# Windowed attention and gated MLP on one core: 24 small dummy products for two wide ones, and packs 2 and 3 regrouped on TensorE

## The chip, the cores and the metric

The kernel runs on one core of a Trainium2 chip, in one launch. The metric is the time of the core on the device in microseconds (us); lower is better. Engines: PE (TensorE, matrix products; PEld is its loading of weights), DVE (VectorE), ACT (ScalarE), POOL (GpSimd), SP (SyncE, which issues most DMAs).

## What is computed

Eight heads of attention over 576 positions for each of 8 batches, each query seeing a window of at most 32 keys (heads 0 to 3: the last 32 positions, heads 4 to 7: every fourth of the last 128), and a gated MLP on the result:

```python
scores = scale * np.matmul(q, k.transpose(0, 1, 3, 2))
scores = np.where(masks[None, :, :, :], scores, -1000000000.0)
scores = scores - np.max(scores, axis=-1, keepdims=True)
attn = np.exp(scores)
attn = attn / (np.sum(attn, axis=-1, keepdims=True) + 1e-09)
x = np.matmul(attn, v).transpose(0, 2, 1, 3).reshape(B * S, H * D)
g = x @ w_gate
out = (g * (1 / (1 + np.exp(-g))) * (x @ w_val)) @ w_out
```

## The kernel before

Attention is cut into packs (PACKS; 4 heads, two times 4 blocks of 32 queries with 64 keys each), numbered m from 0. A pack goes through `scores` (two mask products in bf16, then 32 fp32 products of a 64x32 corner of PE, which the profile shows as 64 records), `shift` (DVE: maximum and subtraction), `exps` (ACT), `turn_e` (four 128x128 transposes on PE into one PSUM bank), `keys` (that bank copied to SBUF, by DVE for the packs in KEYS, else by ACT), `results` (32 fp32 products with v, 64 records), `norm` and `turn_y` (DVE), and `x_copies`, which split the result into two float32r parts (upper by ACT, lower by POOL or DVE) as input x of the MLP.

The MLP goes by items: 256 or 512 tokens by 128 of the 1536 inner columns. An item has 12 gate products (`gv_mm(it, 0)`, bank bg), 12 value products (`gv_mm(it, 1)`, bank bv) and 12 output products (`out_mm`, banks bo0 to bo3); its activation runs on ACT, DVE and POOL. The weights come as 64-bit numbers; each half of an f is loaded by SP, taken apart on ACT and DVE and split into an upper part (ACT cast) and a lower part (POOL, or DVE for the units in W_LOW), unit by unit, while PE works. The first three chunks of 512 tokens are done this way (the first, up to f = 2, as two halves of 256); the rest by a scheme with fewer products, which the change doesn't touch.

The order of the work has two parts. START (line 68) is a hand-written string for the first 16 us: Q are scores, S shift, X exps, T transposes, K keys, A results, N norm, U turn_y, H and L the copies of x, w the loads of weights, W a step of them; I and J are dummy products on a tile of ones, whose output nobody reads (`idle`, lines 812 to 820). After it a recording layer (class Desk, lines 164 to 322) takes down what the loop over the items calls and issues it: PE keeps the order of the calls, the other engines' instructions are ordered by a model of costs and due times, so a change on PE reorders them too. Where in the loop a pack's steps are called stands in EARLY and LATER: three slots for A (results of the pack before, scores of this one), B (transposes and keys) and C (`x_copies`); an item t has slots 3t, 3t + 1 and 3t + 2. Packs 2, 3 and 4 have the rows of EARLY (line 65). All instructions of START show as line L234, those of the recorded part as L250.

```python
EARLY = (-1, 1, None), (2, 4, 3), (5, 8, 6)
```

PE takes its instructions in this order and waits at each for its operands. `two` is the pair of PSUM banks for scores and results: scores at the end of each bank, results at its beginning.

Of the kernel before, what the change touches and what calls it, by code (L numbers as in the profile page):

```python
# [34 lines left out]
BQ = 32  # L35
# [26 lines left out]
WARM = 9  # L62
TURNED = 20
FREE = 16000, 19500, 17500, 18000, 6000
EARLY = (-1, 1, None), (2, 4, 3), (5, 8, 6)
MASKED = 6
X_LOW, W_LOW, H_LOW, KEYS = (3, 7), (1, 5), (5,), (2,)
ON_ACT = (2, 3, 4, 5, 6, 9, 11, 12, 15, 17, 19, 21, 23)
START = ("q0 q1 w v0 v1 w Q0 Q1 S0 X0 T0 W0 I3 I2 S1 K0 X1 W1 A0 W2 T1 J2 K1 W3 J2 N0 W0 w U0 q2 v2 A1 q3 w w r W4 H0 "
         "L0 N1 U1 H1 L1 W1 v3 W2 W3 W4")  # L70
LATER = (14, 3, 2), (23, 3, 4), (29, 7, 4), (39, 3, 2)
T0 = NPLAIN * CH
# [65 lines left out]
NPK = len(PACKS)  # L138
# [15 lines left out]
class Desk:  # L154
# [8 lines left out]
    LANDING, RATE, AHEAD = 2000, 373, 2000  # L163
    EARLY = 6000

# [86 lines left out]
    def issue(self):  # L252
# [7 lines left out]
        for k in range(n - 1, -1, -1):  # L260
            e, _, _, cost, later, _, _ = kept[k]
            way[k] = cost + later + (self.EARLY if later and e == 'scalar' else 0) + max((way[m] for m in after[k]), default=0)
            if e == "tensor":
# [63 lines left out]
def attention_moe(ctx, tc, qkb, vb, w, const, out):  # L327
    nc = Desk(tc.nc)
# [59 lines left out]
    ones = at(M_X0, D)  # L388
# [15 lines left out]
    STAGES = "ETBHL"  # L404
# [6 lines left out]
    def w_load(parts=2):  # L411
        nonlocal loaded
        u = loaded
        n = u % 5 if u < NU - NLAST else (u - NU + NLAST) % NRAW
        if u >= NU or raw_of.get(n, -1) >= done["B" if u < NU - 1 else "L"]:
            return False
        raw_of[n] = u
        loaded += 1
        t = at(raw_at[n], 2 * WU, I32)
        n = 2 * WU // parts  # L420
        for k in range(parts):
            nc.sync.dma_start(out=t[:, n * k:n * k + n], in_=w[u // 2, u % 2].bitcast(I32)[:, n * k:n * k + n])
        t = t.rearrange("p (n t) -> p n t", t=2)
        wst[u] = {"lo": t[:, :, 0], "hi": t[:, :, 1]}
        return True
# [4 lines left out]
    def w_exp(u):  # L430
        y = wst[u]["hi"].bitcast(F32)
        nc.scalar.activation(out=y, in_=y, func=AF.Prelu, scale=2.0 ** -112, alpha=2.0 ** 32)
# [40 lines left out]
    def w_split_hi(u):  # L473
        nc.scalar.copy(out=w_place(u)[0], in_=wst[u].bitcast(F32))
# [5 lines left out]
    ready = {"w": False}  # L480
# [10 lines left out]
    def w_one(c):  # L491
        u = done[c]
        done[c] += 1
        if c == "E":
            w_exp(u)
        elif c == "T":
            w_shift(u)
        elif c == "B":
            w_bits(u)
        elif c == "H":  # L500
            w_split_hi(u)
        else:
            w_split_lo(u)
        if c in "BL":
            while ready["w"] and w_load():
                pass
# [18 lines left out]
    def pool_of(m):  # L525
        return early if m < 2 * NSTART else later
# [24 lines left out]
    def scores(m, two, masked):  # L551

        t = st[m]["qk"]
        if masked:
            for i in range(2):
                nc.tensor.matmul(out=two[:, i, SA:].rearrange("q (g k) -> q g k", g=NG), lhsT=ident16,
                                 rhs=masks_of(m, i), start=True, stop=False, skip_group_check=True)
        for g in range(NG):
            for j in range(NH):
                for i in range(2):  # L560
                    r, q, k = slice(D * i, D * i + D), pk(m).q_at(g, j), pk(m).k_at(i, g, j)
                    nc.tensor.matmul(out=two[BQ * j:BQ * j + BQ, i, SA + BU * g:SA + BU * g + BU],
                                     lhsT=t[r, q:q + BQ], rhs=t[r, k + 1:k + BK], start=not masked,
                                     stop=not masked or g == NG - 1, skip_group_check=True)
# [27 lines left out]
    def turn_e(m, bank):  # L592
        for g in range(NG):
            nc.tensor.transpose(out=bank[:, P * g:P * g + P], in_=st[m]["e"][:, P * g:P * g + P], identity=eye)

    def keys(m, bank, pool):
        t = pool["pt"]()
        if m in KEYS:
            nc.vector.tensor_copy(out=t, in_=bank)
        else:  # L600
            nc.scalar.copy(out=t, in_=bank)
        st[m]["pt"] = t
# [126 lines left out]
    def gv_mm(it, which):  # L729

        text = "Phxw Shxw" if it.w < CH else "phxw shxw"
        if it is not items[0]:
            gv_some(it, which, gv_ops(text), True, True)
        elif which:
            gv_some(it, which, gv_ops("Shwx Phwx"), True, True)
        else:
            gv_some(it, which, gv_ops("Phwx"), True, False)
            attend(-1)
            gv_some(it, which, gv_ops("Shwx"), False, True)
# [30 lines left out]
    def out_mm(it, late=True):  # L770
        f, (_, hh, hl) = it.f, it.h
        ops = [(j, low, x) for j in range(4) for low, x in ((0, hh), (0, hl), (1, hh))]
        if not late:
            ops.sort(key=lambda o: o[2] is hl)
        for n, (j, low, x) in enumerate(ops):
            nc.tensor.matmul(out=bank_o[j][:, it.cols], lhsT=wcol(f, 2 * DM + P * j, low), rhs=x,
                             start=f == it.cols.start == low == 0 and x is hh,
                             stop=f == NF - 1 and j not in [o[0] for o in ops[n + 1:]], skip_group_check=True)
# [19 lines left out]
    two = bank_r = bank(ctx, "two", 2)  # L798
    k_bank = [bank(of_turns, x, 1, "right") for x in ("fk", "fx")] * 2
# [14 lines left out]
    def idle(n, bank=k_bank[1]):  # L814

        while n > 0:
            k = min(n, 4)
            nc.tensor.matmul(out=bank[:D, :P * k].rearrange("p (a b) -> p a b", b=D), lhsT=ones,
                             rhs=ones.unsqueeze(1).broadcast_to([P, 2 * k, D]), start=True, stop=True)
            n -= k  # L820

    idle(WARM)

    items = [Item(0, f, a, a + CH // 2) for a in (0, CH // 2) for f in range(HALVED)]
# [6 lines left out]
        "U": turn_y, "H": lambda m: x_copy(m, "hi"), "L": lambda m: x_copy(m, "lo"),  # L831
        "q": lambda m: load_qk(m, fa, nc.sync, 2),
        "v": lambda m: load_v(m, fa, nc.sync, 2),
        "w": lambda m: w_load(3), "r": lambda m: ready.update(w=True), "I": lambda n: idle(n), "J": lambda n: idle(n, k_bank[0]), "W": lambda n: w_one(STAGES[n]),
    }

    et = mybir.EngineType
# [1 line left out]
    by_hand.__enter__()  # L839
    for what in START.split():  # L840
        first[what[0]](int(what[1:] or 0))
# [14 lines left out]

    for m, x in enumerate(EARLY):
        visits(2 + m, *x)
# [18 lines left out]
    def attend(now):  # L877
        for what, m in visit.get(now, ()):
            r = ended(m)
            if what == "A":  # L880
                if r is not None:
                    results(r, two)
                if m < NPK:
                    scores(m, two, m < MASKED)
                if r is not None:
                    norm(r, two, pool_of(r))
                if m < NPK:
                    shift(m, two, pool_of(m), m < MASKED)
                if r is not None:
                    turn_y(r)  # L890
                if m < NPK:
                    exps(m)
                if 2 * NSTART <= m < TURNED:
                    load_v(m, later, nc.sync)
                elif TURNED <= m - 1 < NPK:
                    load_far(m - 1, later)
                    load_v(m - 1, later, nc.sync)
                if 2 * NSTART <= m + 1 < NPK:
                    load_qk(m + 1, later, nc.sync)
            elif what == "B":  # L900
                if TURNED <= m < NPK:
                    turn_far(m, later)
                elif m < NPK:
                    turn_e(m, two[:, 1])
                    keys(m, two[:, 1], pool_of(m))
            elif r is not None:
                x_copies(r)

# [226 lines left out]
    for t, it in enumerate(items):  # L1135
        before = items[t - 1] if t else None
        late = t >= HALVED
        if it.ci == 0:
            units(it.f)
        gv_mm(it, 0)  # L1140
        act_tanh(it)
        dve_u(it)
        attend(3 * t)
        mixing(t, 0)
        if not late and t:
            out_mm(before, False)
        gv_mm(it, 1)
        dve_h(it)
        h_hi(it)
        if not late:  # L1150
            h_lo(it)
        attend(3 * t + 1)
        if late:
            out_mm(before)
            h_lo(it)
        if t and before.f == NF - 1:
            out_store(before.ci)
        attend(3 * t + 2)
        mixing(t, 1)
        if it.ci == NPLAIN - 1:  # L1160
            if it.f >= 9:
                ask([3, 5, NAT - 1][it.f - 9])
            for n in {6: (0,), 7: (1,), 9: (2, 3), 10: (4, 5), 11: (6, 7)}.get(it.f, ()):
                x_step(n)

    for ci in range(NC):
# [20 lines left out]
        for t in range(NT):  # L1187
            for i in range(NP):
                n = n_out(ci, t, i)
# [59 lines left out]
```

## Time and profile before

| | us |
|---|---|
| median of 3 runs | 911.16 (909.72 to 911.43) |
| the profiled execution, own time | 914.47 |
| its span, first to last instruction | 912.7 |
| PE busy in the span | 897.8 (98%) |
| DVE, ACT, POOL busy | 646.0, 382.5, 257.8 |
| mean granted clock of PE | 0.996 of 2.4 GHz |

The profile is of one execution. Its page gives busy times, the DMA queues and the costliest groups of instructions; the trace behind it answers questions by stretch, engine and time. A row of a timeline merges instructions that follow each other and are alike; an fp32 product is two records, a float32r or bf16 product and a transpose one, and each record has a load of weights (PEld). "[1.89 <-issue]" behind a row is how long the engine was idle before it and what released it.

### The profile page before, as it was taken

Reading aid. Unit: us, or ns where it says so; the run is one execution under the profiler, and the core shown is the slowest. Engines: PE = TensorE matmul, PEld = TensorE weight load, DVE = VectorE, ACT = ScalarE, POOL = GpSimd, SP = SyncE. Lnnn points to the kernel's source line nnn. Section 1 sums busy time; section 2 is a strip of 40 time slices with the busy share of each in tenths; the row PEclk is TensorE's granted clock in tenths of the full one; section 3 lists DMA queues with packets and bytes.
Section 4 is the critical chain, followed back from the end, with each engine's and each line's share of the span. In section 5 each row is a group of like instructions: output and inputs, shape, how many; then the busy total and the mean of one; then the engine's idle time right before and its main releaser. Section 6 shows DMA issues by size and latency. Waiting matters only on the chain.

```text
span 912.7 us, 20897 instructions
## 1 busy us (share of the span) xinstructions
PE 897.8 (98%) x8642; PEld 737.0 (81%) x8642; DVE 646.0 (71%) x993; ACT 382.5 (42%) x593; POOL 257.8 (28%) x177
## 2 busy tenths in 40 slices
PE   6899999999999999999999999999999999999998
PEld 4798888888888888888888888888878888888886
DVE  5687779888795473777789766878787746555752
ACT  4788433333243242333336544333345533334452
POOL 2468712221311112012032630111146501213451
PEclk9899999999999999999999999999999999999999
DMA  9899986453464640887888678989866675565562
GB/s 338 326 337 368 373 287 224 153 184 122 164 239 146 211 162 13 265 288 263 291 272 282 233 247 279 306 279 296 273 211 222 212 240 198 188 199 189 193 223 92
DMA packets 90382, 214.24 MB, mean 235 GB/s; under 512 B 9264, under 2 KB 32432, under 8 KB 90288
## 3 DMA queue, kind: packets, MB, share of 16 engines
q1 hardware_dynamic: 79776, 208.09, 66.2%
q10 hardware_dynamic: 10512, 4.82, 2.0%
q8 instruction: 68, 1.11, 0.5%
q14 instruction: 26, 0.21, 0.1%
HBM read 165.69 MB, written 47.19 MB: 233 GB/s over the span
## 4 chain that ended last, share of the span: by engine, by line
PE 96%; DMA 2%; issue 1%; SPq 0%; ACT 0%; DVE 0%; POOL 0%; ACTq 0%
PE bo L250 43%; PE bg L250 23%; PE bv L250 23%; PE two L250 7%; DMA at_int<-w 1%; DMA at_float<-turned 1%; SPq L234 0%; DVE at_float L250 0%; POOL at_float32r L234 0%; ACT at_float32r L250 0%; ACT at_float32r L234 0%; ACT at_float L250 0%; ACT at_int L234 0%; ACTq L234 0%
## 5 line engine op out<-in xcount | busy, mean ns | idle before, releaser
L250 PE MATMUL bo<-at_float32r 128*128 128x512 f32 x1296 | 305.7, 390 | 0.0
L250 PEld LDWEIGHTS bo<-at_float32r 128*128 128x128 f32 x1296 | 242.6, 188 | 51.0
L250 POOL TENSOR_TENSOR at_float32r<-at_float,at_float32r 128x512 fp32r<-128x512 f32 (+1 forms) x109 | 161.0, 1480 | 388.7 <-ACT at_float32r L250 210.4
L250 ACT CAST at_float32r<-at_float 128x512 fp32r<-128x512 f32 (+2 forms) x214 | 147.9, 705 | 146.6 <-DVE at_float L250 69.9
L250 DVE TENSOR_TENSOR at_float<-bo,at_float 128x512 f32<-128x512 f32 x168 | 114.1, 683 | 99.7 <-ACT at_float L250 63.7
L250 DVE TENSOR_TENSOR at_float32r<-at_float,at_float32r 128x512 fp32r<-128x512 f32 (+1 forms) x105 | 108.9, 1051 | 48.2 <-ACT at_float32r L250 38.1
L250 PE MATMUL bv<-at_float32r 128*128 128x512 f32 x486 | 128.6, 391 | 0.0
L250 PE MATMUL bg<-at_float32r 128*128 128x512 f32 x486 | 128.3, 390 | 0.0
L250 ACT ACTIVATE at_float<-at_float 128x512 f32<-128x512 f32 (+1 forms) x108 | 67.9, 630 | 134.7 <-DVE at_float L250 121.4
L250 PE MATMUL bg<-at_float32r,at_float32r 128*128 128x512 f32 (+1 forms) x468 | 108.8, 382 | 1.8 <-ACT at_float32r L234 1.2
L250 POOL TENSOR_TENSOR at_float<-at_float,at_float 128x512 f32<-128x512 f32 x36 | 51.3, 1424 | 209.8 <-DVE at_float L250 190.8
L250 PE MATMUL bv<-at_float32r,at_float32r 128*128 128x512 f32 (+1 forms) x468 | 107.2, 379 | 0.0
L250 DVE SCALAR_TENSOR_TENSOR at_float<-at_float,at_float 128x512 f32<-128x512 f32 x144 | 106.1, 743 | 1.1
L250 PE MATMUL bo<-at_float32r,at_float32r 128*128 128x512 f32 (+1 forms) x468 | 106.8, 377 | 0.0
L250 PEld LDWEIGHTS bg<-at_float32r 128*128 128x128 f32 x486 | 90.9, 188 | 19.1
L250 PEld LDWEIGHTS bv<-at_float32r 128*128 128x128 f32 x486 | 90.8, 188 | 19.2
L250 PEld LDWEIGHTS bg<-at_float32r,at_float32r 128*128 128x128 f32 x468 | 83.7, 192 | 18.5 <-ACT at_float32r L234 1.4
L250 PEld LDWEIGHTS bv<-at_float32r,at_float32r 128*128 128x128 f32 x468 | 83.3, 191 | 15.8
L250 PEld LDWEIGHTS bo<-at_float32r,at_float32r 128*128 128x128 f32 x468 | 82.8, 188 | 16.4 <-POOL at_float32r L250 0.2
L250 ACT COPY at_float<-bg 128x512 f32<-128x512 f32 x63 | 37.0, 587 | 84.8 <-PE bg L250 79.9
L250 DVE TENSOR_TENSOR at_float<-at_float,at_float 128x512 f32<-128x512 f32 (+2 forms) x80 | 63.8, 806 | 2.4 <-POOL at_float L250 1.2
L250 ACT COPY at_float<-bv 128x512 f32<-128x512 f32 x63 | 37.1, 589 | 36.9 <-PE bv L250 36.1
(73 smaller groups left out, 610.0 us busy)
## 6 DMA issues: line engine op xcount, KB each, us to landing
at_float32r<-pieces SPq DMA_DIRECT2D x189, 512.0 KB, 4.2
pieces<-at_float32r SPq DMA_DIRECT2D x126, 256.0 KB, 4.2
at_float<-qkb SPq DMA_DIRECT2D x32, 576.0 KB, 6.2
at_float<-vb SPq DMA_DIRECT2D x34, 520.0 KB, 5.4
at_int<-w SPq DMA_DIRECT2D x38, 384.0 KB, 6.2
out<-at_float SPq DMA_DIRECT2D x36, 256.0 KB, 4.3
turned<-at_float SPq DMA_DIRECT2D x18, 256.0 KB, 4.8
at_float<-turned ACTq DMA_DIRECT2D x72, 64.0 KB, 5.2
```

What stands on the lines that cost most here:

```text
L250: self.kept.append([engine, lambda: f(*a, **k), sorted(m for m in after if m >= 0), cost, later, both, start])
```

## The change

- In START the two dummy products of 256 columns (J2, twice) behind the transposes of pack 1 become two times 12 products of 32x32 (G12, function `tiny`).
- The transposes of pack 2 go into bank bo3 instead of `two`, and its keys are copied from there (BEFORE = 3).
- Pack 3's scores are called before the results of pack 2 instead of behind them.
- Pack 3's transposes are called in front of the value products of item 1 (slot 3.5, a new call of `attend`) instead of behind them.

```diff
@@ -62,11 +62,12 @@
 WARM = 9
 TURNED = 20
 FREE = 16000, 19500, 17500, 18000, 6000
-EARLY = (-1, 1, None), (2, 4, 3), (5, 8, 6)
+EARLY = (-1, 1, None), (2, 3.5, 3), (5, 8, 6)
+BEFORE = 3
 MASKED = 6
 X_LOW, W_LOW, H_LOW, KEYS = (3, 7), (1, 5), (5,), (2,)
 ON_ACT = (2, 3, 4, 5, 6, 9, 11, 12, 15, 17, 19, 21, 23)
-START = ("q0 q1 w v0 v1 w Q0 Q1 S0 X0 T0 W0 I3 I2 S1 K0 X1 W1 A0 W2 T1 J2 K1 W3 J2 N0 W0 w U0 q2 v2 A1 q3 w w r W4 H0 "
+START = ("q0 q1 w v0 v1 w Q0 Q1 S0 X0 T0 W0 I3 I2 S1 K0 X1 W1 A0 W2 T1 G12 K1 W3 G12 N0 W0 w U0 q2 v2 A1 q3 w w r W4 H0 "
          "L0 N1 U1 H1 L1 W1 v3 W2 W3 W4")
 LATER = (14, 3, 2), (23, 3, 4), (29, 7, 4), (39, 3, 2)
 T0 = NPLAIN * CH
@@ -819,6 +820,10 @@
                              rhs=ones.unsqueeze(1).broadcast_to([P, 2 * k, D]), start=True, stop=True)
             n -= k
 
+    def tiny(n, bank):
+        for _ in range(n):
+            nc.tensor.matmul(out=bank[:BQ, :BQ], lhsT=ones[:, :BQ], rhs=ones[:, :BQ], start=True, stop=True)
+
     idle(WARM)
 
     items = [Item(0, f, a, a + CH // 2) for a in (0, CH // 2) for f in range(HALVED)]
@@ -831,7 +836,7 @@
         "U": turn_y, "H": lambda m: x_copy(m, "hi"), "L": lambda m: x_copy(m, "lo"),
         "q": lambda m: load_qk(m, fa, nc.sync, 2),
         "v": lambda m: load_v(m, fa, nc.sync, 2),
-        "w": lambda m: w_load(3), "r": lambda m: ready.update(w=True), "I": lambda n: idle(n), "J": lambda n: idle(n, k_bank[0]), "W": lambda n: w_one(STAGES[n]),
+        "w": lambda m: w_load(3), "r": lambda m: ready.update(w=True), "G": lambda n: tiny(n, k_bank[0]), "I": lambda n: idle(n), "W": lambda n: w_one(STAGES[n]),
     }
 
     et = mybir.EngineType
@@ -878,9 +883,11 @@
         for what, m in visit.get(now, ()):
             r = ended(m)
             if what == "A":
+                if m == BEFORE:
+                    scores(m, two, m < MASKED)
                 if r is not None:
                     results(r, two)
-                if m < NPK:
+                if m < NPK and m != BEFORE:
                     scores(m, two, m < MASKED)
                 if r is not None:
                     norm(r, two, pool_of(r))
@@ -901,8 +908,9 @@
                 if TURNED <= m < NPK:
                     turn_far(m, later)
                 elif m < NPK:
-                    turn_e(m, two[:, 1])
-                    keys(m, two[:, 1], pool_of(m))
+                    turned_at = bank_o[3] if m == BEFORE - 1 else two[:, 1]
+                    turn_e(m, turned_at)
+                    keys(m, turned_at, pool_of(m))
             elif r is not None:
                 x_copies(r)
 
@@ -1144,6 +1152,7 @@
         mixing(t, 0)
         if not late and t:
             out_mm(before, False)
+        attend(3 * t + 0.5)
         gv_mm(it, 1)
         dve_h(it)
         h_hi(it)
```

What that does to PE at the dummies (tiles at_64_float are the ones; fk, fx and two PSUM banks; the last 32x65 are the results of pack 1), before:

```order
L234 MATMUL fx<-at_64_float_62 64x256
L234 MATMUL two<-at_1040_float_149,at_512_float_241 32x65 x32
L234 MATMUL fx<-at_192_bfloat_61,at_512_float_126 128x128 x4
L234 MATMUL fk<-at_64_float_62 64x256 x2
L234 MATMUL two<-at_1040_float_152,at_512_float_284 32x65 x32
L250 MATMUL bg<-at_1024_float32r,at_1536_float32r 128x256 x6
```

and in the changed kernel:

```order
L235 MATMUL fx<-at_64_float_62 64x256
L235 MATMUL two<-at_1040_float_149,at_512_float_241 32x65 x32
L235 MATMUL fx<-at_192_bfloat_61,at_512_float_126 128x128 x4
L235 MATMUL fk<-at_64_float_62 32x32 x24
L235 MATMUL two<-at_1040_float_152,at_512_float_295 32x65 x32
L251 MATMUL bg<-at_1024_float32r,at_1536_float32r 128x256 x6
```

Two instructions became 24 in the same place, between the transposes and the results of pack 1; nothing else moved here.

PE from the value products of item 0 to the results of pack 3, before (bg, bv, bo are the banks of gate, value and output; 32x63 are scores, 32x65 results, 128x252 masks, 128x128 transposes; of the output products between only the last is shown, and one of the two mask products):

```order
L250 MATMUL bv<-at_1024_float32r,at_1536_float32r 128x256 x12
L250 MATMUL two<-at_192_bfloat_61,at_512_float_124 128x128 x4
L250 MATMUL two<-at_1040_float_149,at_512_float_241 32x65 x32
L250 MATMUL two<-at_384_bfloat_60 128x252
L250 MATMUL two<-at_1280_float_142 32x63 x32
L250 MATMUL bg<-at_1024_float32r,at_1536_float32r 128x256 x12
L250 MATMUL bo_394<-at_512_float32r,at_1536_float32r 128x256
L250 MATMUL bv<-at_1024_float32r,at_1536_float32r 128x256 x12
L250 MATMUL two<-at_192_bfloat_61,at_512_float_126 128x128 x4
L250 MATMUL two<-at_1040_float_152,at_512_float_284 32x65 x32
```

and in the changed kernel:

```order
L251 MATMUL bv<-at_1024_float32r,at_1536_float32r 128x256 x12
L251 MATMUL bo_416<-at_192_bfloat_61,at_512_float_124 128x128 x4
L251 MATMUL two<-at_384_bfloat_60 128x252
L251 MATMUL two<-at_1280_float_142 32x63 x32
L251 MATMUL two<-at_1040_float_149,at_512_float_241 32x65 x32
L251 MATMUL bg<-at_1024_float32r,at_1536_float32r 128x256 x12
L251 MATMUL bo_416<-at_512_float32r,at_1536_float32r 128x256
L251 MATMUL two<-at_192_bfloat_61,at_512_float_126 128x128 x4
L251 MATMUL bv<-at_1024_float32r,at_1536_float32r 128x256 x12
L251 MATMUL two<-at_1040_float_152,at_512_float_295 32x65 x32
```

The transposes of pack 2 write bo3, the scores of pack 3 stand between them and the results of pack 2, and the transposes of pack 3 stand ahead of the value products instead of behind.

ACT around its copy of the keys of pack 3 (COPY from `two`; CAST to at_1536_float32r are upper halves of weights, ACTIVATE from bg the tanh of item 1), before:

```order
L250 ACTIVATE at_1536_int_145<-at_1536_int_145 128x768
L250 ACTIVATE at_512_float_445<-bg 128x256
L250 ACTIVATE at_1536_int_145<-at_1536_int_145 128x768
L250 CAST at_1536_float32r<-at_776_int_358 128x768
L250 COPY at_512_float_284<-two 128x512
L250 CAST at_1536_float32r<-at_776_int_450 128x768
```

and in the changed kernel:

```order
L251 ACTIVATE at_1536_int_363<-at_1536_int_363 128x768
L251 ACTIVATE at_1536_int_145<-at_1536_int_145 128x768
L251 COPY at_512_float_295<-two 128x512
L251 CAST at_1536_float32r<-at_776_int_380 128x768
L251 ACTIVATE at_512_float_467<-bg 128x256
L251 ACTIVATE at_1536_int_145<-at_1536_int_145 128x768
```

The copy, which waits for the transposes of pack 3, now stands ahead of that cast of weights and of the tanh of item 1, both of which stood ahead of it.

## Rows read from the trace of the kernel before

**Rows 1.** The page: busy time of PE and its loads; packets, MB, share of q8.
```profile
PE 897.8 (98%) x8642; PEld 737.0 (81%) x8642; DVE 646.0 (71%) x993; ACT 382.5 (42%) x593; POOL 257.8 (28%) x177
...
q8 instruction: 68, 1.11, 0.5%
```

**Rows 2.** Windows: length, each engine's busy us (count), granted clock, DMA share, GB/s.
```profile
core 0: us, PE busy (x) PEld busy (x) DVE busy (x) ACT busy (x) POOL busy (x), PEclk, DMA share, GB/s
22.80:26.20 3.40, 2.79 (x14) 2.38 (x12) 2.03 (x4) 3.01 (x5) 1.34 (x1) 0.51 1.03 389
30.00:33.00 3.00, 3.00 (x40) 2.83 (x41) 2.14 (x5) 0.81 (x2) 0.49 (x1) 0.50 1.02 413
33.10:40.00 6.90, 6.22 (x166) 5.59 (x166) 4.75 (x8) 5.70 (x10) 3.35 (x3) 1.00 0.55 210
40.00:912.00 872.00, 868.10 (x7963) 715.47 (x7961) 622.49 (x950) 359.45 (x560) 244.75 (x163) 1.00 0.68 230
```

**Rows 3.** Timeline of PE, 13 to 41 us: start, us, operation, records [idle <-releaser].
```profile
13.09 1.08 PE L234 MATMUL fk<-at_float 128*64 128x256 f32 x4
14.32 1.06 PE L234 MATMUL two<-at_float,at_float 64*32 64x65 f32 x64
...
18.61 0.81 PE L250 MATMUL two<-at_float 64*32 64x63 f32 x59
21.30 0.30 PE L250 MATMUL two<-at_float 64*32 64x63 f32 x5 [1.89 <-issue]
...
24.53 1.06 PE L250 MATMUL two<-at_bfloat,at_float 128*128 128x128 f32 x4
26.37 0.86 PE L250 MATMUL two<-at_float,at_float 64*32 64x65 f32 x64 [0.78 <-DVE at_float L250]
...
27.48 0.57 PE L250 MATMUL two<-at_float 64*32 64x63 f32 x35
30.00 0.66 PE L250 MATMUL two<-at_float 64*32 64x63 f32 x29 [1.95 <-issue]
30.60 2.78 PE L250 MATMUL bg<-at_float32r,at_float32r 128*128 128x256 f32 x12
...
34.65 1.60 PE L250 MATMUL bv<-at_float32r,at_float32r 128*128 128x256 f32 x12
...
37.36 0.86 PE L250 MATMUL two<-at_float,at_float 64*32 64x65 f32 x64 [0.68 <-ACT at_float L250]
...
39.26 1.70 PE L250 MATMUL bg<-at_float32r,at_float32r 128*128 128x256 f32 x12
```

**Rows 4.** DMA in windows 11-12.15, 18.75-19.85, 27.4-28.55, 33.8-35, 38.8-40; last 26.4-26.9.
```profile
q8 instruction: 1, 0.02, 5.9%
...
q8 instruction: 1, 0.02, 6.0%
...
q8 instruction: 1, 0.02, 5.7%
...
q8 instruction: 1, 0.02, 5.4%
...
q8 instruction: 1, 0.02, 5.8%
...
at_float<-qkb SPq DMA_DIRECT2D x1, 576.0 KB, 7.7
```

**Rows 5.** Timeline of DVE: norm of pack 0, weights' lower half, maximum of pack 2.
```profile
13.53 0.69 DVE L234 TENSOR_TENSOR at_float<-two,at_float 128x512 f32<-128x512 f32 x1
...
20.02 1.31 DVE L234 TENSOR_TENSOR at_float32r<-at_int,at_float32r 128x768 fp32r<-128x768 f32 x1 [0.90 <-ACT at_float32r L234]
...
21.65 0.68 DVE L250 TENSOR_REDUCE at_float<-two 128x8 f32<-128x504 f32 x1 [0.32 <-PE two L250]
```

**Rows 6.** Timeline of ACT: exponentials of pack 2, cast of the weights' fifth half.
```profile
23.15 0.62 ACT L250 ACTIVATE at_float<-at_float 128x504 f32<-128x504 f32 x1 [0.21 <-DVE at_float L250]
...
34.68 0.84 ACT L250 CAST at_float32r<-at_int 128x768 fp32r<-128x768 f32 x1
```

**Rows 7.** Timeline of POOL: the lower half of the same weights.
```profile
35.60 1.84 POOL L250 TENSOR_TENSOR at_float32r<-at_int,at_float32r 128x768 fp32r<-128x768 f32 x1 [5.11 <-ACT at_float32r L250]
```

## The prediction

> **What bounds the kernel.** I read the page first: the tensor engine PE is busy for 897.8 of 912.7 us, and one queue (q8) brings only instructions, 68 packets for 17,284 PE records, one per 254, or about 128 products with their weight loads [rows 1]. Then the stretches: from 40 to 912 us PE misses 3.9 us of 872, so 11 of the 14.9 that it misses in all lie before 40 us [rows 2]. There I followed PE's timeline [rows 3]. Two holes are marked "issue" (PE waits for nothing the profile shows): 1.89 us inside the scores of pack 2, after 59 of 64 records, and 1.95 us inside those of pack 3, after 35 of 64 (packs are counted from 0, so the diff's third and fourth are 2 and 3). Between the holes stand 5 + 6 + 12 + 4 + 64 + 2 + 35 = 128 products: exactly one q8 packet. So the holes are waits for code. The packets stand in 18.75 to 19.85 and 27.4 to 28.55 [rows 4]; PE goes on at 21.30 and 30.00, 1.45 us after each packet both times. What starts a packet can be read too: PE passes the edge one block earlier at 14.35 (59 + 2 + 6 products back from hole 1, 3 into the results of pack 1), at 21.30 and at 30.00, and the next packet comes 4.4, 6.1 and 3.8 us later [rows 3, 4], in line behind the data that fill the queues (share 1.03 and 1.02 in 22.8 to 33, [rows 2]). A code block is requested when the engine enters the block before it.
>
> **The change, part by part.** All times are those of the profiled execution: span 912.7, own time 914.47, which is 3.3 above the median of the runs shown, 911.16; a difference in it is carried over to that median.
>
> 1. *Code edges.* Of the fp32 products each is two records with a load each: two become 24, so 22 x 4 = 88 more PE instructions, 44 records with loads. Every edge therefore comes 44 records earlier in the work: the edge before hole 1 goes from 3 records into the results of pack 1 to record 7 of the 48 dummies, hole 1 to 15 records into the scores of pack 2. By the new order the second hole is then 49 + 6 + 12 + 4 + 2 + 55 records on: after 55 of 64 scores of pack 3.
>
> 2. *The dummies.* The old four records took 1.08 us, 0.27 each at 256 columns. For 32 columns no row exists: above, by columns, 0.034 each, 1.6 us for 48; below, the pace of the scores, 0.81/59 = 0.014, 0.7 us. I take 0.028 (1.3 us), nearer the first, because the dummies fill all 128 rows as the old ones do and scores use a 64x32 corner. Begun at 13.09, they meet the code edge at 13.3; its packet stands at 11.0 to 12.15, plus 1.45 is usable at 13.6; 41 records more end at 14.7. The results of pack 1 started at 14.32, held by DVE's norm until 14.22 [rows 5]. Cost 0.4 at that place, 0 to 0.7 by the bounds. The Trainium skill, "TensorE: Matmul & The Clock Gate", section "Wait — 56ns, not 53.3ns?", gives a floor of about 25 ns from start to start however few columns; by it the 48 records would be an estimated 1.2 us, and the cost 0.3.
>
> 3. *Hole 1.* PE now enters the earlier block at 13.6 in place of 14.3, 0.7 sooner, because the dummies stand ahead of the wait for DVE. With the same delay in the queue the code is usable at 21.30 - 0.7 = 20.6. PE reaches the edge at 18.85, so the hole is 1.75 against 1.89; 49 records at 0.014 follow, and the scores end at 21.3, before at 21.6. Gain 0.3.
>
> 4. *Up to the transposes of pack 2.* DVE's lower half of the weights (20.02, 1.31 us) hangs on the results of pack 1 and moves by up to 0.4, to 21.7; its maximum then starts where it did, 21.65, and the exponentials end at about 23.85 (23.77 before) [rows 5, 6]. PE's 18 gate and value products end at 23.4 to 24.2, by the clock: in 22.8 to 26.2, behind hole 1, it was granted 0.51, the 1.2 GHz level [rows 2]. So the transposes start at 24.0, before 24.53, and end at 24.4. Gain 0.5.
>
> 5. *Regrouping.* They now go to bank bo3 and the scores of pack 3 follow without the 0.78 wait for DVE's copy. That gains nothing yet: after 2 masks and 55 records PE stands at the next edge at 25.5. Its code was requested at 20.6. With the packet (1.1 us) and 1.45 behind it, the longest delay, 6.1, which was seen at this very place, gives 20.6 + 6.1 + 2.5 = 29.2, the shortest, 3.8, 27.0; I take 29.0, near the delay seen here. The hole grows to 3.5 us, but behind it only 9 scores and the results (0.86) are left: the gate products of the next item start at 30.0 to 30.1, before 30.60. Gain 0.5.
>
> 6. *The transposes of pack 3* stand ahead of the value products, so ACT's copy of their keys lies beside the value products (1.60) and the 0.68 wait before the results goes [rows 3]. I let the lower clock (0.50 in 30 to 33, [rows 2]) come back after the hole as it did; it doubles the gate group, 2.78 against 1.70. Results of pack 3: 36.1 in place of 37.36. Gain 1.3 in all.
>
> 7. *What is late next.* ACT now has the cast of the next weights (0.84) behind that copy, and POOL's 1.84 behind the cast [rows 6, 7]: with 0.7 for the copy, ready 3.4 us after the transposes. PE needs them after value, results, scores and four gate products, 1.5 + 0.9 + 1.1 + 0.5 = 4.0 us. Cover 0.6, cost 0; uncovered it would be paid in full. SP's load of pack 4's v waits for the results of pack 2, which now end 2 us later; a load issued after 26.4 took 7.7 us to land [rows 4], so the queues have other data meanwhile: cost 0. The next edge lies 14 records into the results of pack 3, the one after that at the end of the next gate group (39.7). The first is requested at 29.0 and needed at 36.3: nothing. The second is requested at 36.3. In 33.1 to 40 the queues are only 0.55 busy [rows 2]; in the old trace the packet of that stretch stands from 38.8 on, 0.7 after PE entered the block (59 records into the results of pack 3, 38.1, [rows 3, 4]). So 36.3 + 0.7 + 1.1 + 1.45 = 39.5: cost 0, bound 1. From 40 us PE is full as before, and the order differs on the other engines only, which have room (DVE 622 of 872 us, [rows 2]).
>
> Sum: -1.3 us, 911.16 - 1.3 = **909.9**.
>
> **Rivals.**
> *A, the forecast*, both holes stay and move: 0.5 to 1.9 faster. Chance 0.52.
> *B, the second request is served sooner*, after 3.8 us as after 30.00. Code at 27.0, gate products at 28.0; if PE's shorter rest then also spares the lower clock, 1 us more. Bound: the scores of pack 4 can't start before about 34.2 (their load was issued after 26.4 and took 7.7 us [rows 4]), so at most 39.26 - 35.1 = 4.1. I price it at 3.4: 907.8. For it: the delays differ by 2.3 us. Against: the longest was measured at just this place. Chance 0.28.
> *C, slower: the hole comes back at the edge behind the gate group of item 2.* Results and scores of packs 3 and 4 run 128 small records between two edges within 4 us. Requested at 36.3, code comes a delay and 2.5 us later; a delay over 39.7 - 36.3 - 2.5 + 1.3 = 2.2 us eats the gain; with the longest, 6.1, it is code at 44.9, a hole of 5.2, 3.9 slower: 915.1. For it: delays of 3.8 to 6.1 are the rule while the queues are full. Against: they drain here. Chance 0.10.
> *D, the holes don't follow the count of instructions*, and only the last 0.7 less the dummies' 0.4 remains: 910.9. The 128 products between the holes speak against it. The Trainium skill's "Runtime: NRT & Kernel Launch", section "Instruction fetch mechanics", has PE hold 2048 instructions in blocks of 256, the fetch mostly hidden, and by it a shift of 88 would move nothing; the block size agrees with the 254 records per packet here, the hiding doesn't agree with the two holes. Chance 0.10.
>
> **Numbers.** A measurement of this kernel tells about 0.2%, 1.8 us, from no change: under 909.3 is faster, over 913.0 slower. A gives 0.11 of faster, B 0.25: 0.36. C gives 0.08 slower, from a delay of 4 us on. The rest, 0.56, is no difference. The range 907.3 to 912.0 takes in A with its bounds and most of B, and leaves out the far ends of B and C.
>
> **What would show it.** In the changed profile: "issue" holes after about 15 of 64 scores of pack 2 and 55 of 64 of pack 3, 128 products apart; the first ending near 20.6, the second near 29; dummies at 0.028 us each with a rest near 13.3; results of pack 1 near 14.7; no wait before the results of pack 3; gate products of item 2 near 38.0 in place of 39.26. Holes at other counts make the reading of the code edges wrong; a second hole ending before 27.5 makes B right; a hole after 39 us makes C right.

## The result and the profile after

The change makes the kernel slower: 917.08 us as the median of 8 runs (914.75 to 920.68) against 910.99 for the kernel before in the same comparison, a ratio of 1.0073 with a 95% interval of 1.0051 to 1.0095, or 6.6 us on 911. The forecast was 909.9 in 907.3 to 912.0: the direction is wrong and the range does not hold the time. The profiled execution of the changed kernel took 916.81 us, close to its median; its span is 914.9. (In the table further down the ratio is the one of the comparison, with its interval, and not the quotient of the two medians; where the two differ the ratio counts.)

The page of the changed kernel, the lines that answer to [rows 1]:

```profile
PE 898.7 (98%) x8686; PEld 737.0 (81%) x8686; DVE 653.0 (71%) x993; ACT 382.0 (42%) x593; POOL 260.8 (29%) x177
...
q8 instruction: 69, 1.13, 0.5%
```

PE has 44 records more, as counted, and one code packet more. Its busy time is 0.9 us up, so most of the 6 us is not work.

The timeline of PE, start of the changed kernel (columns as in [rows 3]):

```profile
13.18 1.45 PE L235 MATMUL fk<-at_float 128*32 128x32 f32 x40 [0.35 <-issue]
14.56 0.86 PE L235 MATMUL two<-at_float,at_float 64*32 64x65 f32 x64
...
18.47 1.11 PE L251 MATMUL two<-at_float 64*32 64x63 f32 x64
...
24.27 0.85 PE L251 MATMUL two<-at_float 64*32 64x63 f32 x64
...
29.72 0.63 PE L251 MATMUL two<-at_bfloat,at_float 128*128 128x128 f32 x4 [0.76 <-DVE at_float L251]
...
33.62 0.85 PE L251 MATMUL two<-at_float 64*32 64x63 f32 x64 [0.72 <-DMA at_float<-qkb]
34.40 1.58 PE L251 MATMUL bg<-at_float32r,at_float32r 128*128 128x256 f32 x11
37.42 0.28 PE L251 MATMUL bg<-at_float32r,at_float32r 128*128 128x256 f32 x1 [1.44 <-issue]
37.53 1.60 PE L251 MATMUL bo<-at_float32r,at_float32r 128*128 128x256 f32 x12
```

Both holes of [rows 3] in the scores of packs 2 and 3 are gone in this trace: 64 records in one row each time (the first row takes 1.11 us, 0.26 more than the second; see e5). The gate group of item 2 starts at 34.40 in place of 39.26, 4.9 us sooner than in the profile of before. One new hole follows at once, 1.44 us, inside that gate group, after 11 of its 12 products. The queues were full there, unlike in [rows 2], where their share was 0.55 in the same stretch (columns as there):

```profile
33.10:40.00 6.90, 4.95 (x97) 4.76 (x98) 5.49 (x10) 5.88 (x9) 3.11 (x3) 1.00 1.01 369
```

The edge one block earlier lies 128 records ahead of the hole, 13 records into the results of pack 3, at about 31.9. No code packet stands in 31.8 to 35, one stands in 35.0 to 36.15: the request waited some 3.1 us.

The rest is lost much later. The same view near 650 us, where the results of one pack and the scores of another follow each other (some rows of one to three records between them are left out):

```profile
649.64 0.80 PE L251 MATMUL two<-at_float,at_float 64*32 64x65 f32 x60
...
650.30 0.83 PE L251 MATMUL two<-at_float 64*32 64x63 f32 x62
651.06 0.73 PE L251 MATMUL bo<-at_float32r 128*128 128x512 f32 x2
653.59 6.89 PE L251 MATMUL bo<-at_float32r 128*128 128x512 f32 x22 [1.80 <-issue]
660.32 1.52 PE L251 MATMUL bg<-at_float32r 128*128 128x512 f32 x6
```

Another hole for code: 1.80 us, after the pair (128 records, each with its load: 256 instructions) and two more products. So a code edge lies on the first records of the pair, and the next one, 256 instructions on, just behind it: the whole block runs in 651.79 - 649.64 = 2.15 us, and its successor is not there. Behind the hole 22 products take 660.32 - 653.59 = 6.7 us. The reason that it is so long is the clock, in the view by stretches (columns as in [rows 2]):

```profile
17.60:24.20 6.60, 5.06 (x92) 4.00 (x92) 5.36 (x8) 4.83 (x7) 2.15 (x2) 1.00 1.05 391
...
653.50:660.30 6.80, 6.71 (x22) 5.38 (x23) 4.40 (x9) 1.62 (x3) 0.00 (x0) 0.75 0.40 134
```

In 653.5 to 660.3 the mean granted clock is 0.75, so about half of the stretch is at the 1.2 GHz level; in 17.6 to 24.2 it is the full 2.4 GHz (in the kernel before it was 0.51 in 22.8 to 26.2, [rows 2]).

Last, what PE waited for from 40 to 912 us (total, times, longest), where the trace of the kernel before has only one wait for a transfer of `turned`, 0.7 us, and a second trace of it (e0 below) three, 1.6 us together:

```profile
PE bo L251 <- issue: 2.0, 2, 1.8
PE two L251 <- DMA at_float<-turned: 1.3, 3, 0.7
PE two L251 <- ACT at_float L251: 0.5, 1, 0.5
```

### The profile page after: what moved, and what is told of

Its sections match the earlier page's. It is cut to its first block, busy times and chain, and to the rows that moved or that the text cites. A ratio compares the mean times of both kernels' runs of the same rounds, so it can differ in the third digit from the quotient of the medians.

```text
span 914.9 us, 20987 instructions
## 1 busy us (share of the span) xinstructions
PE 898.7 (98%) x8686; PEld 737.0 (81%) x8686; DVE 653.0 (71%) x993; ACT 382.0 (42%) x593; POOL 260.8 (29%) x177
## 4 chain that ended last, share of the span: by engine, by line
PE 90%; DMA 6%; DVE 2%; issue 1%; SPq 0%; ACT 0%; DVEq 0%; ACTq 0%
PE bo L251 41%; PE bv L251 22%; PE bg L251 22%; PE two L251 6%; DMA at_int<-w 2%; DVE at_float L251 2%; DMA at_float<-turned 2%; DMA at_float<-qkb 1%; DMA at_float<-vb 1%; DMA turned<-at_float 0%; DVE at_float32r L251 0%; DMA pieces<-at_float32r 0%; SPq L251 0%; ACT at_float L251 0%; ACT at_float32r L251 0%
## 5 line engine op out<-in xcount | busy, mean ns | idle before, releaser
L251 POOL TENSOR_TENSOR at_float32r<-at_float,at_float32r 128x512 fp32r<-128x512 f32 (+1 forms) x109 | 163.3, 1500 | 397.0 <-ACT at_float32r L251 243.9
L251 PEld LDWEIGHTS bg<-at_float32r,at_float32r 128*128 128x128 f32 x468 | 82.6, 188 | 18.9 <-POOL at_float32r L235 1.4
```

Of the source, the lines that this page charges most:

```text
L251: self.kept.append([engine, lambda: f(*a, **k), sorted(m for m in after if m >= 0), cost, later, both, start])
```

## Experiments

The table gathers them. "Ratio" is to the kernel before on the same chip, "us" the ratio taken on 910. "Code holes" are "issue" holes of PE behind 30 us in that kernel's trace, with the place.

| kernel | median us | ratio (95%) | us | code holes behind 30 us |
|---|---|---|---|---|
| the change | 917.08 | 1.0073 (1.0051 to 1.0095) | +6.6 | 1.44 at 36, 0.2 at 55, 1.80 at 652 |
| e1 dummies alone | 915.48 | 1.0065 (1.0043 to 1.0086) | +5.9 | 2.77 at 36, 0.2 at 57, 1.19 at 655 |
| e2 regrouping alone | 911.11 | 1.0008 (0.9994 to 1.0023) | +0.7 | none |
| e3 change, 4 dummies fewer | 912.45 | 1.0023 (1.0005 to 1.0040) | +2.1 | 0.65 at 37 |
| e4 change, 3 dummies more | 916.54 | 1.0058 (1.0036 to 1.0080) | +5.3 | 2.40 at 35, 0.2 at 55, 3.28 at 652 |
| e5 change, edge moved at 635 us | 914.56 | 1.0030 (1.0014 to 1.0047) | +2.7 | 2.24 at 36 |
| e6 before, 88 instructions at 540 us | 916.03 | 1.0042 (1.0020 to 1.0064) | +3.8 | 1.73 at 651 |
| e7 regrouping, two wide dummies | 911.13 | 0.9989 (0.9970 to 1.0008) | -1.0 | 0.16 at 33 |
| e8 regrouping, no dummies | 911.19 | 1.0005 (0.9989 to 1.0021) | +0.5 | 1.26 at 566 |
| e9 regrouping, one wide dummy | 910.69 | 0.9997 (0.9987 to 1.0007) | -0.3 | none |

### The kernel before once more (e0)

No edit. 

> The kernel before once more, for a second trace of it. Its first profiled execution took 914.5 us, 3.5 above the median of its runs, with two code holes of 1.89 and 1.95 us ahead of 31 us and with PE at the 1.2 GHz level for some 6.5 us behind them. Theory 1: a usual execution of 911 us has the same two holes after the same counts of records, but shorter ones (the requests are served sooner) or without the lower clock. Theory 2: the 3.5 us lie after 40 us.

It took 911.20 us, in one execution; the kernel before had a median of 909.86 in that comparison. PE's timeline of this second trace:

```profile
18.77 1.49 PE L250 MATMUL two<-at_float 64*32 64x63 f32 x64
...
26.70 0.85 PE L250 MATMUL two<-at_float 64*32 64x63 f32 x64
...
35.08 1.69 PE L250 MATMUL bg<-at_float32r,at_float32r 128*128 128x256 f32 x12
36.61 1.60 PE L250 MATMUL bo<-at_float32r,at_float32r 128*128 128x256 f32 x12
...
647.87 0.80 PE L250 MATMUL two<-at_float,at_float 64*32 64x65 f32 x60
...
649.28 5.75 PE L250 MATMUL bo<-at_float32r 128*128 128x512 f32 x24
654.87 1.52 PE L250 MATMUL bg<-at_float32r 128*128 128x512 f32 x6
```

and the stretch behind the start of the recorded part, of the same trace:

```profile
17.60:24.20 6.60, 6.60 (x87) 5.77 (x88) 4.90 (x7) 5.00 (x8) 2.10 (x2) 0.50 1.05 392
```

Neither hole is there. The packet with the code for the scores of pack 2 stood in 17.2 to 18.4, not from 18.75 on [rows 4], and the lower clock came earlier (0.50 from 17.6 to 24.2), so PE took 1.49 us for these scores: the code was in time. The gate group of item 2 starts at 35.08, 4.2 us before the 39.26 of [rows 3]. So theory 2 falls, and theory 1 is right that the difference lies ahead of 40 us, but not in its form: the holes are not shorter, they are absent. The trace on which the forecast was built shows an execution 3.5 us above its median, and those microseconds are the two holes that the forecast wanted to shorten.

Against this trace the change reads like this. Gate group of item 2: 34.40 - 35.08 = -0.7. The output group behind it: 37.53 - 36.61 = +0.9, so the hole at 36 us costs 1.6. The pair near 650: 649.64 - 647.87 = +1.8, that is 0.85 more, of which 0.2 for code and 0.5 for ACT are in the waits above; the waits for `turned` ahead of the pair go the other way (0.6 here, 1.0 in e0), and the rest is not placed. The gate group behind the pair: 660.32 - 654.87 = +5.45, so this one place costs 3.7: the hole of 1.80, and 22 products in 6.7 us where 24 took 5.59 here (22/24 of it is 5.1), 1.6 for the clock. The spans differ by 5.5, the medians by 6.1.

### The dummies alone (e1)

```diff
-T1 J2 K1 W3 J2 N0
+T1 G12 K1 W3 G12 N0
```

> The 24 small dummies alone, nothing regrouped. Theory 1 (every code edge behind the dummies moves 88 PE instructions ahead, and one of them, near 650 us, comes to lie on the first records of a pair of results and scores whose 256 records are a whole code block): the hole of about 1.8 us near 650 us is there as in the changed kernel, with the lower clock behind it; the first 40 us gain 1 to 3 us; so the time is 911 to 915. Theory 2 (the regrouping and the new order on DVE, ACT and POOL cost the time): no hole near 650 us, and the time within 1 us of the kernel before.

915.48 us, +5.9 by the ratio: theory 1, just above its range. The two holes in its timeline, and the gate group of item 3 behind the first:

```profile
34.10 1.57 PE L250 MATMUL bg<-at_float32r,at_float32r 128*128 128x256 f32 x11
38.45 0.30 PE L250 MATMUL bg<-at_float32r,at_float32r 128*128 128x256 f32 x1 [2.77 <-issue]
...
43.28 1.68 PE L250 MATMUL bg<-at_float32r,at_float32r 128*128 128x256 f32 x12
...
656.01 5.53 PE L250 MATMUL bo<-at_float32r 128*128 128x512 f32 x23 [1.19 <-issue]
```

The holes stand in the same groups as in the changed kernel, and nothing was regrouped. The 24 dummies bring nearly the whole loss. It is shared out in another way in this trace, and not as theory 1 had it. The start does gain 1.0 us (34.10 against e0's 35.08), but the hole at 36 us takes more than that: the gate group of item 3 starts at 43.28, 3.4 us behind e0's 39.84, so that place costs 4.4. Behind the hole near 650 us PE had the full clock (1.00 in 656.01 to 661.38), and the place costs 1.5 us (661.38 - 652.90 = 8.48 from the start of the pair to the gate group behind it, 7.00 in e0), where it costs 3.7 in the changed kernel.

### The regrouping alone (e2)

```diff
-T1 G12 K1 W3 G12 N0
+T1 J2 K1 W3 J2 N0
```

> The regrouping of packs 2 and 3 alone, with the two dummies of 256 columns. Theory 1: the code edges stay where they were, so there is no hole near 650 us; a hole of about 1.9 us stays in the scores of pack 2 after 59 records, the second falls into the results of pack 2; the wait for DVE ahead of the results and the wait for ACT's copy are gone; 907.5 to 910.5 us. Theory 2: the order on the other engines costs the time behind 50 us: 913 to 917.

911.11 us, ratio 1.0008 with 1 inside its interval: no difference that can be measured. Theory 2 falls. Theory 1 was right that no hole stands near 650 us, but the two holes that it left in the start did not come, and it was too hopeful of the gain. The gate group of item 2 starts at 33.49, 1.6 before the 35.08 of e0, and the pair near 650 us at the same time as in e0. In its timeline, and what PE waited for from 30 us on:

```profile
33.49 1.70 PE L251 MATMUL bg<-at_float32r,at_float32r 128*128 128x256 f32 x12
...
647.88 0.80 PE L251 MATMUL two<-at_float,at_float 64*32 64x65 f32 x60
```

```profile
PE two L251 <- DMA at_float<-turned: 0.9, 2, 0.6
PE two L251 <- ACT at_float L251: 0.8, 1, 0.8
...
PE bg L251 <- DVE at_float32r L251: 0.3, 1, 0.3
```

What is gained in the start is gone by 650 us. Between the two rows PE waits 1.4 us here (0.8 for ACT, 0.3 for DVE, 0.3 for `turned`; the longer wait for `turned` comes later) and 1.0 in e0, all for `turned`. That places 0.4 of the 1.6 us; the rest is not placed.

### Four dummies fewer, three more (e3, e4)

```diff
-T1 G12 K1 W3 G12 N0
+T1 G12 K1 W3 G8 N0     (e3)
+T1 G12 K1 W3 G15 N0    (e4)
```

> The changed kernel with 12 and 8 small dummies in place of 12 and 12, so 16 PE instructions fewer. Theory 1: every edge comes 16 records later; at 650 us the block then ends 8 products of the next group (8 x 0.24 us = 1.9 us) later, which covers the hole of 1.80, and the lower clock behind it (1.5 us) goes too; the hole of 1.44 us in the gate group of item 2 at 36 us moves to behind that group's end and shrinks to 0.4: 911.5 to 913.5 us against 917.1. Theory 2 (the hole near 650 us isn't set by the count of instructions): it stays, 916 to 918.

912.45 us, as theory 1 put it, and the holes moved as counted (its "16 records" are 16 instructions: 8 records, each with its load). In e3:

```profile
35.88 1.00 PE L251 MATMUL bo<-at_float32r,at_float32r 128*128 128x256 f32 x7
37.53 0.76 PE L251 MATMUL bo<-at_float32r,at_float32r 128*128 128x256 f32 x5 [0.65 <-issue]
...
649.50 5.75 PE L251 MATMUL bo<-at_float32r 128*128 128x512 f32 x24
```

16 instructions fewer put the early hole 8 products on, from 11 of 12 gate products to 7 of 12 output products, and it shrank from 1.44 to 0.65; the late one is gone.

> The changed kernel with 12 and 15 small dummies, so 12 PE instructions more. The edge that lay on the third product of the pair of results and scores near 650 us then lies 4 value products ahead of the pair, in front of the pair's wait for its transposed input. Theory 1a (the request goes out when PE's sequencer, which runs ahead of the work, passes the edge; the wait at the head of the pair stopped it): the request goes out some microseconds earlier, no hole near 650 us, the lower clock behind it gone (together 3.3 us less); the hole near 36 us grows by 6 gate products, 0.8 us: 914 to 915.5. Theory 1b (the sequencer isn't ahead): the block still holds 248 of the 256 small records, a hole of about 1 us and the lower clock stay, and with the larger hole near 36 us: 916.5 to 918.

916.54 us. The trace speaks against theory 1a, and 1b is right in kind, too small in the size of the hole. But the trace is of the slowest of the ten executions (919.77): five took 914.25 to 915.07, which is 1a's range, and five 918.02 to 919.77, so what happened near 650 us in the shorter five is not shown. In e4:

```profile
37.64 0.99 PE L251 MATMUL bg<-at_float32r,at_float32r 128*128 128x256 f32 x7 [2.40 <-issue]
...
655.65 0.42 PE L251 MATMUL two<-at_float 64*32 64x63 f32 x4 [3.28 <-issue]
656.01 7.97 PE L251 MATMUL bo<-at_float32r 128*128 128x512 f32 x24
```

The early hole stands 6 products sooner and has grown by 1.0. The late hole is now inside the scores, four records before the end of the pair, 6 records ahead of its old place, and it grew to 3.28. The edge one block earlier lies among the value products, near 649.5; the code packet stands in 653.3 to 654.3, nearly 4 us later. In the changed kernel the edge is passed at about 649.65 and the packet stands in 650.6 to 652.2, 1 us later. The queues at the time of the request and behind it, e4:

```profile
649.00:650.00 1.00, 1.00 (x7) 0.81 (x6) 0.10 (x1) 0.59 (x1) 0.00 (x0) 1.00 0.90 221
...
651.00:652.00 1.00, 1.00 (x106) 1.00 (x110) 0.75 (x2) 0.75 (x2) 0.00 (x0) 1.00 0.53 156
```

and the changed kernel:

```profile
649.00:650.00 1.00, 1.00 (x40) 0.61 (x40) 0.69 (x1) 0.26 (x1) 0.00 (x0) 1.00 0.63 254
```

The share of 0.90 against 0.63 goes with the longer delay, but e4's request also waited through a stretch of 0.53. Why it waited so long stays open.

### The late edge alone, taken away and put in (e5, e6)

```diff
 def results(m, two):
 ...
-    for n in range(NH * NG):
+    for n in [0] * (4 if m == 34 else 0) + list(range(NH * NG)):     (e5, in the changed kernel)
+    for n in [0] * (11 if m == 28 else 0) + list(range(NH * NG)):    (e6, in the kernel before)
```

> The changed kernel with the first two products of the results near 635 us issued four times more (32 PE instructions, the same values written again). Everything ahead of 635 us stays as it was; the edge at 650 us moves 32 records ahead, out of the pair. Theory 1 (code edges): the hole of 1.8 us near 650 us and the lower clock behind it go, 3.3 us, for 0.4 us of products: 913.5 to 915. Theory 2 (the hole comes from something else): 917 to 918.

914.56 us, theory 1; by the ratios 6.6 - 2.7 = 3.9 us come back though the kernel does more work, and the two intervals do not overlap. The edit moves every edge behind 635 us; no code hole is left there, and the output group behind the pair runs through:

```profile
650.72 5.73 PE L251 MATMUL bo<-at_float32r 128*128 128x512 f32 x24
```

The trace shows something else too. Up to 635 us this kernel has the changed kernel's instructions, and in this execution a hole for code does stand in the scores of pack 2, after 15 of 64 records, the very place that the forecast had counted out:

```profile
18.12 0.34 PE L251 MATMUL two<-at_float 64*32 64x63 f32 x15
19.40 0.94 PE L251 MATMUL two<-at_float 64*32 64x63 f32 x49 [0.94 <-issue]
```

> The kernel before with the first two products of the results near 540 us issued eleven times more: 88 PE instructions, as many as the change adds, but not at the start. Everything up to there is the kernel before. Theory 1: the edge at 650 us comes to lie on the third product of the pair, as in the changed kernel: a hole of 1 to 2 us there, perhaps with the lower clock behind it; with 1.2 us for the products 912 to 915 against 909.9. Theory 2 (the hole hangs on what the change does at the start): no hole, 911 to 911.5.

916.03 us, +3.8 by the ratio. Theory 2, whose price was the products alone, falls all the more, since that price was put too high: 22 products are 44 records with 44 loads, at 0.0135 us a record 0.6 us, not 1.2. In e6:

```profile
649.36 0.81 PE L250 MATMUL two<-at_float,at_float 64*32 64x65 f32 x60
...
653.01 5.51 PE L250 MATMUL bo<-at_float32r 128*128 128x512 f32 x23 [1.73 <-issue]
```

This is the kernel before up to 540 us, with its old start and no regrouping, and the hole of the changed kernel stands at the pair near 650 us. The place of the edge is the cause of the hole, whatever put it there. In this trace the clock stayed up behind it:

```profile
653.01:658.36 5.35, 5.35 (x24) 4.43 (x24) 4.10 (x9) 1.31 (x3) 0.00 (x0) 1.00 0.59 202
```

So the place costs 2.0 us here (658.36 - 649.36 = 9.00 from the start of the pair to the gate group behind it, 7.00 in e0), and with 0.6 for the products some 1.2 of the 3.8 are not placed.

### What the dummies are good for (e7, e8, e9)

```diff
-T1 G12 K1 W3 G12 N0
+T1 J4 K1 W3 J4 N0     (e7)
+T1 K1 W3 N0           (e8)
+T1 J4 K1 W3 N0        (e9)
```

> The regrouping with two dummies of 512 columns in place of the 24 small ones: as much dummy work for PE, but as many instructions as before. Theory 1: the edges lie as in the kernel before, no hole near 36 or 650 us; PE stays at 2.4 GHz from 16 to 24 us as in the changed kernel, and what that gives is lost to the waits for weights, exponentials and loads: 909 to 911.5. Theory 2 (the clock in the start is worth its 2 us at the end): 907 to 908.5.

911.13 us, ratio 0.9989, 1 inside the interval: theory 1. From 17.6 to 24.2 us PE is at full clock, where e0 had 0.50, and is busy for 4.3 us in place of 6.6:

```profile
17.60:24.20 6.60, 4.26 (x87) 3.47 (x86) 5.63 (x7) 4.37 (x6) 2.54 (x2) 1.00 1.04 383
```

Yet the gate group of item 2 starts at 35.08, as in e0, and 1.6 us later than in e2 (33.49), which has the same grouping and a mean granted clock of 0.54 in that stretch. Its timeline, and what PE waited for from 13 to 36 us:

```profile
35.08 1.69 PE L251 MATMUL bg<-at_float32r,at_float32r 128*128 128x256 f32 x12
```

```profile
PE two L251 <- issue: 1.8, 3, 1.0
PE bo L251 <- ACT at_float L251: 0.9, 1, 0.9
```

At the full clock PE uses its code up sooner, and waits for it and for the exponentials of pack 2 (ACT) instead.

> The regrouping with no dummies behind the transposes of pack 1 at all: 8 PE instructions fewer than the kernel before, so every edge lies 8 records later in the work; counted against the pairs of results and scores, none lies in the first 20 records of a pair behind 80 us. Theory 1 (the dummies give nothing at the end, since the start waits for weights, exponentials and loads; what counts is where the edges lie): no code hole behind 40 us, 909 to 911 against 910. Theory 2 (the dummies keep the clock up and that is worth its time): 911.5 to 914.

911.19 us, ratio 1.0005: theory 2 falls, but theory 1's count of the edges missed one:

```profile
562.47 0.81 PE L251 MATMUL two<-at_float,at_float 64*32 64x65 f32 x60
...
567.74 0.73 PE L251 MATMUL bo<-at_float32r 128*128 128x512 f32 x2 [1.26 <-issue]
```

The hole stands 10 output products behind the pair, 2 ahead of the end of that group of 12, so the edge lies some 10 records with their loads, 20 instructions, inside the pair; the expectation had taken 20 for the end of the danger and counted loads as records. From the edge (about 562.6) to the code it took 5.1 us, where the changed kernel's hole near 650 us shows 3.9 (649.65 to 653.59): the later the code comes, the wider the zone.

> The regrouping with one dummy of 512 columns, 4 PE instructions fewer than the kernel before. Theory 1: as with no dummies, no code hole behind 40 us, 909 to 911. Theory 2: between that kernel and the one with two dummies of 512 columns.

910.69 us, ratio 0.9997 (0.9987 to 1.0007), no code hole behind 40 us: theory 1. None of the versions beats the kernel before by more than its interval.

## Why the prediction was wrong, step by step

1. *Code edges* (step 1). Right as a mechanism and in the places at the start where a hole shows the edge: the rest in the dummies stands after 8 of 48 records and ends at 13.18 (forecast 13.6), the hole in e5 stands after 15 of 64 scores of pack 2, and the hole in the gate group of item 2, after 11 of 12 products, is the edge that rival C named. What failed is where the counting stopped. 88 instructions move *all* edges, nearly 70 packets' worth, and the forecast looked at those ahead of 40 us alone.
2. *Step 7 is the step that failed*, with both of its terms. *"From 40 us PE is full as before"* put the edges behind 40 us at nothing, and no rival had them: in this trace the pair near 650 us alone costs 3.7 us, a hole of 1.80 and some 1.6 for the lower clock behind it (e5 gives 3.9 us back by the ratios; e6 makes the hole without the rest of the change). *"Cost 0, bound 1"* for the edge at the gate group of item 2 took a delay of 0.7 us from a stretch where the queues were 0.55 busy; in the changed kernel they were 1.01 busy there, the packet came some 3.1 us behind the edge, and the hole cost 1.6 us in this trace, in e1's, with a lower clock behind it, 4.4. By the rule that the prediction quoted from the Trainium skill, "Runtime: NRT & Kernel Launch", section "Instruction fetch mechanics" (fetch mostly hidden), e6 would have cost its 0.6 us of products; it cost 3.8, with a hole of 1.73 us for code.
3. *The base* ("a difference in it is carried over to that median"). The gain of 1.3 us was to come out of two holes that e0 does not have. Measured against e0 the start gains 0.7 us at the gate group of item 2, not the 4.9 that the two first profiles show. A kernel whose profiled execution lies 3.5 us above its median was showing something that the usual run lacks; the forecast noted the difference and did not ask where it lay.
4. *The dummies* (step 2): 40 records from 13.18 to 14.56, 0.0345 each. Forecast 0.028; it is the upper bound, the price by columns. The floor of about 25 ns from start to start that the prediction quotes from the Trainium skill ("TensorE: Matmul & The Clock Gate", section "Wait — 56ns, not 53.3ns?") does not hold for all small products here: the scores run at 0.81/59 = 0.014 us a record ([rows 3]). The results of pack 1 start at 14.56, forecast 14.7; that they agree is luck, since the code came 0.4 us sooner than forecast and the records took longer.
5. *Holes 1 and 2* (steps 3 to 5): neither came in this trace, beyond the 0.26 us in the scores of pack 2; in e5 hole 1 came at the forecast place, 0.94 us long, forecast 1.75. That the requests are served sooner, as rival B had it for the second, is what these traces show: the packets stand in 16.3 to 17.6 and 22.3 to 23.6, so the requests at about 13.2 (in the dummies) and 18.9 (15 records into the scores of pack 2) waited some 3 to 3.5 us, not 4.4 and 6.1.
6. *Transposes of pack 3 early* (step 6): the 0.68 wait ahead of the results is gone. But the transposes wait 0.76 for DVE, and the next scores 0.72 for their load, which the prediction had as the bound of rival B (34.2; they start at 33.62).
7. *Rival C* (step 7, "cost 0, bound 1"): it came, at its place, 1.44 us in this trace, 2.2 to 2.8 in e1, e4 and e5 (e4 at an edge 6 products earlier). The price of its hole, 5.2, was too high; as it came in all four traces of kernels with 24 or 27 small dummies, its chance of 0.10 was too low.

What stays open: e3 has one code hole of 0.65 and the span of its trace is 0.4 us below e0's, yet its ratio is 1.0023. One trace per kernel doesn't place the last one or two microseconds, and how the loss is shared between 36 and 650 us differs from trace to trace. The rest of the loss in e5 (2.7) goes with the hole at 36 us, which no run took away alone.

## What to carry to other kernels

A code block here is 256 instructions, so 128 small records with their loads use one up in some 2 us, while its successor came 3.1 to 6.1 us behind the edge in the late holes here (3.1 in e1, 3.6 in e6, 3.9 in the changed kernel, 5.1 in e8, 6.1 in e4). A wait marked "issue" in the middle of a burst, 128 records behind the edge before it, is such a wait. When a change adds or removes instructions on PE, count the edges through the whole program, and look at every burst of small products, not only at the stretch that was edited. Adding tiny products to fill a gap is dear in this currency: the two wide dummies of e7 kept PE busy for 1.93 us with 8 instructions, the 24 tiny ones of the change for 0.44 + 1.45 us with 96.

Before a forecast takes a gain out of a profile, compare the profiled execution's time with the median; when they differ by more than the expected gain, take a second trace first.

## What the runs showed of the hardware that was not expected

- The lower clock behind a code hole is not certain: a hole of 1.80 us was followed by 0.75 mean granted clock in the changed kernel, one of 1.73 us by the full clock in e6.
- A block's delay is not a fixed number at one place: the two traces of the same kernel have the packet for the scores of pack 2 in 17.2 to 18.4 and from 18.75 on, and the gate group of item 2 starts 4.2 us apart in them.
- PE at 2.4 GHz in place of 1.2 over 6.6 us of the start (e7 against e0, which differ by the regrouping too) left the gate group of item 2 at the same 35.08; against e2, with e7's grouping and the lower clock, it starts 1.6 us later.
